# A SwiGLU kernel on one core: w2 in one load, the last token tile stored as 384 and 128 columns

## The chip, the cores and the metric

One Trainium2 chip, one core. The metric is the device time of one execution in microseconds (us); the time of a kernel is the median of several executions. TensorE does the matrix products, ScalarE the sigmoid and some of the copies out of PSUM, VectorE the multiplications and the rest of the copies, and SyncE's queue (SP) issues nearly all DMA transfers.

## The reference

```
B, S, D, F = 32, 32, 512, 1792        # x [B,S,D], w1 and w3 [D,F], w2 [F,D], all bf16
gate = einsum("bsd,df->bsf", x, w1)
up   = einsum("bsd,df->bsf", x, w3)
h    = silu(gate) * up
out  = einsum("bsf,fd->bsd", h, w2)   # 1024 tokens x 512
```

## The kernel before

The 1024 tokens stand in two blocks of 512 (`NB`) for the projections and in eight tiles of 128 (`NT`) for the output. F is cut into 14 pieces of 128 (`FT`).

**Loads.** At the start SP issues, in program order: a part of x, the first three F pieces of w1 and w3, a transposing load of x (line 78), the rest of w1 and w3 in three steps (`load_w`, line 66), a second transposing load for token block 1 (line 82), and last w2 in two halves of seven F pieces each (lines 84 and 85). Two loads go through ScalarE's queue. That makes 16 loads.

**Projections.** For each token block and each F piece, four matmuls make `gate_ps` and four make `up_ps` (`project`, line 123); `swiglu` takes the sigmoid on ScalarE (line 133) and multiplies twice on VectorE (lines 135 and 136) into `hT`, which holds h with F on the partitions.

**Output.** For each token tile `nt`, 14 matmuls (line 176) add up 128 tokens x `DB` columns in one PSUM tile `o_ps`, `hT` being the stationary operand and `w2_sb` the moving one. For the first seven tiles `DB` is 512, ScalarE casts `o_ps` to bf16 in `o_sb` (line 187), and SP stores it (line 188, 128 KB). The last tile is done in three pieces of 256, 128 and 128 columns, one after the other, each with its own 14 matmuls, a cast on VectorE (line 185) and a store (64, 32 and 32 KB). That makes ten stores, 26 transfers in all.

**What sets the order.** The program is in manual order: each engine runs its instructions in the order written, and waits on semaphores where it needs another engine's result. The `o_sb` tiles rotate over three buffers, so a cast also waits for the store that last used its buffer; the `o_ps` tiles rotate over four PSUM buffers. The DMA transfers take eight completion semaphores in turn, in program order: the first transfer takes semaphore 0, the ninth takes semaphore 0 again, and each transfer waits until the one eight before it has landed. These semaphores are called lane 0 to lane 7 below.

**The end.** After the last store SP waits for all lanes. This is a row of five wait instructions on SP (line 218 in the profile), with up to two semaphores each. In the program of the kernel before they are, in order: lane 3; lanes 4 and 2; lanes 5 and 1; lanes 6 and 0; lane 7 and VectorE. A drain and a barrier of all engines follow, and the span ends.

Of the kernel before, what the change touches and what calls it, by code (L numbers as in the profile page):

```python
# [10 lines left out]
def kernel(  # L11
# [8 lines left out]
    nc = tc.nc  # L20
# [5 lines left out]
    B, S, D = x.shape  # L26
# [5 lines left out]
    FT = F // P  # L32
# [8 lines left out]
    w2_v = w2.rearrange("(ft p) d -> p ft d", p=P)  # L41
# [14 lines left out]
    w2_sb = consts.tile([P, FT, D], bf16, name="w2_sb")  # L56
# [23 lines left out]
        load_w(nc.sync, w1_sb, w1_v, c0, c1)  # L80
        load_w(nc.sync, w3_sb, w3_v, c0, c1)
    nc.sync.dma_start_transpose(out=xT[:, :, NB:N], in_=x_flat[NB:N, :])
    FH = FT // 2
    nc.sync.dma_start(out=w2_sb[:, 0:FH, :], in_=w2_v[:, 0:FH, :])
    nc.sync.dma_start(out=w2_sb[:, FH:FT, :], in_=w2_v[:, FH:FT, :])

    def bank(name, tag="any"):
        return psum.tile([P, NB], fp32, name=name, tag=tag)
# [81 lines left out]
    for nt in range(NT):  # L170
        last = nt == NT - 1
        c0 = 0
        for DB in (D // 2, D // 4, D // 4) if last else (D,):
            o_ps = psum.tile([P, DB], fp32, name="o_ps", tag="any")
            for fo in range(FT):
                nc.tensor.matmul(  # L176
                    o_ps[:],
                    lhsT=hT[:, fo, nt * P : (nt + 1) * P],
                    rhs=w2_sb[:, fo, c0 : c0 + DB],
                    start=(fo == 0),  # L180
                    stop=(fo == FT - 1),
                )
            o_sb = work.tile([P, DB], bf16, name="o_sb", tag="o_sb")
            if last:
                nc.vector.tensor_copy(o_sb[:], o_ps[:])  # L185
            else:
                nc.scalar.copy(o_sb[:], o_ps[:])  # L187
            nc.sync.dma_start(
                out=out_flat[nt * P : (nt + 1) * P, c0 : c0 + DB],
                in_=o_sb[:],  # L190
            )
            c0 += DB
# [30 lines left out]
```

## Time and profile before

| what | value |
|---|---|
| median of five executions | 82.9 us |
| the five executions | 82.66, 82.71, 82.90, 83.63, 84.78 us |
| the profiled execution's own time | 83.63 us |
| its span | 81.8 us (81.84 in the trace) |
| TensorE busy | 76.3 us, 93% of the span |
| VectorE, ScalarE busy | 40.5 us, 22.9 us |
| granted TensorE clock | full in every slice |
| DMA moved | 7.67 MB |

The span is what the profile sees of the device's work. The profiled execution's own time is 1.79 us longer (83.63 - 81.84), which lies around it. That execution is also 0.73 us above the median of the five. A busy TensorE is a modelled figure, since matmuls are pipelined: the pace of the matmuls is read from the distance between their starts.

### The profile page before, as it was taken

The page shows a single profiled execution, that of the slowest core. Times are in us where ns is not written, and L with a number is a line of the kernel's source. Part 1 is how long each engine was busy: PE and PEld are TensorE (multiplying, and loading weights), DVE is VectorE, ACT ScalarE, POOL GpSimd, SP SyncE. Part 2 cuts the span into 40 slices and gives each one's busy share as a digit, 9 for nine tenths or more (in the row PEclk, how much of TensorE's full clock was granted, in tenths as well). Part 3 has the DMA queues.
Part 4 walks back from the last instruction along what each step waited for, and adds up shares of the span by engine and source line. Part 5 has one row for each costly group of instructions (what it writes and reads, how often), then busy time and mean ns, then how long its engine had stood idle before and what let it go on. Part 6 is the DMA issues. An engine that isn't in the chain of part 4 may idle for free.

```text
span 81.8 us, 1049 instructions
## 1 busy us (share of the span) xinstructions
PE 76.3 (93%) x396; PEld 38.1 (47%) x402; DVE 40.5 (49%) x62; ACT 22.9 (28%) x39; POOL 0.7 (1%) x6
## 2 busy tenths in 40 slices
PE   6989949999999999999999999999999999999960
PEld 2468714444444444444444444444444444444850
DVE  0130699678878778788788887883000000000040
ACT  4410721442224432234322244220220220220200
POOL 3000000000000000000000000000000000000000
PEclk9999999999999999999999999999999999999999
DMA  1999999978991000000000000000011012011120
GB/s 17 308 287 300 345 334 346 170 167 209 347 342 39 0 0 0 0 0 0 0 12 0 0 0 0 0 4 0 0 64 64 15 50 72 24 41 64 40 72 16
DMA packets 10949, 7.67 MB, mean 94 GB/s; under 512 B 3776, under 2 KB 10944, under 8 KB 10944
## 3 DMA queue, kind: packets, MB, share of 16 engines
q1 hardware_dynamic: 10528, 7.28, 32.9%
q10 hardware_dynamic: 416, 0.33, 1.2%
q8 instruction: 3, 0.05, 0.2%
q14 instruction: 2, 0.02, 0.1%
HBM read 5.77 MB, written 1.05 MB: 83 GB/s over the span
## 4 chain that ended last, share of the span: by engine, by line
PE 81%; DMA 9%; SPq 4%; issue 1%; DVE 0%; DVEq 0%
PE o_ps L176 30%; PE up_ps L123 26%; PE gate_ps L123 25%; DMA w_sb<-in_w_dram 9%; SPq L66 2%; SPq L78 2%; SPq L62 0%; DVE o_sb L185 0%; DVEq L185 0%
## 5 line engine op out<-in xcount | busy, mean ns | idle before, releaser
L123 PEld LDWEIGHTS <-w_sb 128*128 128x128 bf16 x248 | 24.0, 98 | 26.1 <-DMA w_sb<-in_w_dram 2.5
L123 PE MATMUL gate_ps<-xT,w_sb 128*128 128x512 bf16 (+1 forms) x122 | 28.7, 358 | 1.3 <-DMA w_sb<-in_w_dram 1.2
L123 PE MATMUL up_ps<-xT,w_sb 128*128 128x512 bf16 (+1 forms) x122 | 28.7, 358 | 0.5 <-DMA w_sb<-in_w_dram 0.5
L133 ACT ACTIVATE sig<-gate_ps 128x512 f32<-128x512 f32 x28 | 16.7, 597 | 33.2 <-PE gate_ps L123 33.2
L176 PE MATMUL o_ps<-w_sb,hT 128*128 128x512 bf16 (+2 forms) x138 | 24.3, 336 | 0.1
L135 DVE TENSOR_TENSOR t<-gate_ps,sig 128x512 f32<-128x512 f32 x28 | 19.3, 691 | 9.9 <-ACT sig L133 9.9
L136 DVE TENSOR_TENSOR hT<-t,up_ps 128x512 bf16<-128x512 f32 x28 | 19.3, 688 | 2.9
L176 PEld LDWEIGHTS <-hT 128*128 128x128 bf16 x140 | 12.6, 98 | 12.0
L185 DVE CAST o_sb<-o_ps 128x128 bf16<-128x128 f32 (+1 forms) x3 | 1.0, 337 | 22.3 <-PE o_ps L176 22.3
L187 ACT CAST o_sb<-o_ps 128x512 bf16<-128x512 f32 x7 | 4.1, 586 | 17.9 <-PE o_ps L176 17.9
L94 PE MATMUL warm_ps<-const-bfloat16-1.0 128*128 128x512 bf16 x6 | 2.7, 623 | 0.8 <-PEq L207 0.8
L116 DVE CAST xT<-pT 128x256 bf16<-128x256 f32 (+1 forms) x3 | 1.1, 380 | 3.8 <-PE pT L106 3.7
L74 ACT ACT_TABLE_LOAD x1 | 1.3, 1283 | 1.2 <-PEq L207 1.2
L94 PEld LDWEIGHTS <-const-bfloat16-1.0 128*128 128x128 bf16 x6 | 0.7, 133 | 1.9 <-issue 1.9
L106 PEld LDWEIGHTS <-x_sb 128*128 128x128 bf16 x8 | 0.8, 135 | 0.8 <-DMA x_sb<-in_x_dram 0.8
L106 PE MATMUL pT<-ident,x_sb 128*128 128x128 bf16 x8 | 1.1, 307 | 0.0
L116 ACT CAST xT<-pT 128x128 bf16<-128x128 f32 (+1 forms) x2 | 0.6, 319 | 1.3 <-PE pT L106 1.3
masks.py:199 POOL TENSOR_SCALAR_AFFINE_SELECT ident<-ident 128x128 bf16<-128x128 bf16 x1 | 0.3, 292 | 0.1
masks.py:197 POOL MEMSET ident<- 128x128 bf16 x1 | 0.2, 204 | 0.3 <-POOLq L207 0.3
L74 ACT ACTIVATE table<-const-bfloat16-1.0 128x1 f32<-128x1 bf16 x1 | 0.2, 202 | 0.0
L207 POOL MEMSET const-uint8-127<- 128x1 uint8 x1 | 0.1, 103 | 0.0
L207 POOL MEMSET const-bfloat16-1.0<- 128x1 bf16 x1 | 0.1, 102 | 0.0
(2 smaller groups left out, 0.2 us busy)
## 6 DMA issues: line engine op xcount, KB each, us to landing
w_sb<-in_w_dram SPq DMA_DIRECT2D x4, 512.0 KB, 7.8
w_sb<-in_w_dram SPq DMA_DIRECT2D x2, 896.0 KB, 6.9
out_dram<-o_sb SPq DMA_DIRECT2D x7, 128.0 KB, 1.7
w_sb<-in_w_dram SPq DMA_DIRECT2D x2, 384.0 KB, 8.6
w_sb<-in_w_dram SPq DMA_DIRECT2D x3, 192.0 KB, 3.9
w_sb<-in_w_dram ACTq DMA_DIRECT2D x1, 192.0 KB, 3.8
x_sb<-in_x_dram ACTq DMA_DIRECT2D x1, 128.0 KB, 2.7
x_sb<-in_x_dram SPq DMA_DIRECT2D x1, 128.0 KB, 2.6
```

The source lines that it names most:

```text
L66: queue.dma_start(out=w_sb[:, d0:d1, f0:f1], in_=w_v[:, d0:d1, f0:f1])
L74: nc.scalar.activation(table[:], one, SIGMOID)
L78: nc.sync.dma_start_transpose(out=xT[:, :, HB:NB], in_=x_flat[HB:NB, :])
L94: nc.tensor.matmul(warm_ps[:, 0:cols], lhsT=one.to_broadcast([P, P]), rhs=one.to_broadcast([P, cols]), start=True, stop=True,)
L106: nc.tensor.matmul(pT[:, i, j, :], lhsT=x_sb[:, nt, dt * P : (dt + 1) * P], rhs=ident[:], start=True, stop=True,)
L116: copy(xT[:, dts[0] : dts[-1] + 1, nts[0] * P : (nts[-1] + 1) * P], pT[:].rearrange("p d t c -> p d (t c)"),)
L123: nc.tensor.matmul(ps[:, c0 : c0 + n1 - n0], lhsT=w_sb[:, dt, fo * P : (fo + 1) * P], rhs=xT[:, dt, n0:n1], start=(dt == 0), stop=(dt == D ...
L133: nc.scalar.activation(sig[:], gate_ps[:], SIGMOID)
L135: nc.vector.tensor_mul(t[:], gate_ps[:], sig[:])
L136: nc.vector.tensor_mul(hT[:, fo, nb * NB : (nb + 1) * NB], t[:], up_ps[:])
L176: nc.tensor.matmul(o_ps[:], lhsT=hT[:, fo, nt * P : (nt + 1) * P], rhs=w2_sb[:, fo, c0 : c0 + DB], start=(fo == 0), stop=(fo == FT - 1),)
L187: nc.scalar.copy(o_sb[:], o_ps[:])
```

## The change

The two loads of w2 become one load of 1,792 KB. The last token tile is done in two pieces, of 384 and 128 columns, instead of three. The first piece is cast by ScalarE, as the tiles before it are; only the last piece (`c0 > 0`) is cast by VectorE. There are 15 loads and nine stores, 24 transfers in all. Lines after the w2 load stand two lines earlier in the changed kernel.

```diff
@@ -80,9 +80,7 @@
         load_w(nc.sync, w1_sb, w1_v, c0, c1)
         load_w(nc.sync, w3_sb, w3_v, c0, c1)
     nc.sync.dma_start_transpose(out=xT[:, :, NB:N], in_=x_flat[NB:N, :])
-    FH = FT // 2
-    nc.sync.dma_start(out=w2_sb[:, 0:FH, :], in_=w2_v[:, 0:FH, :])
-    nc.sync.dma_start(out=w2_sb[:, FH:FT, :], in_=w2_v[:, FH:FT, :])
+    nc.sync.dma_start(out=w2_sb[:], in_=w2_v)
@@ -170,7 +168,7 @@
     for nt in range(NT):
         last = nt == NT - 1
         c0 = 0
-        for DB in (D // 2, D // 4, D // 4) if last else (D,):
+        for DB in (D - D // 4, D // 4) if last else (D,):
             o_ps = psum.tile([P, DB], fp32, name="o_ps", tag="any")
             for fo in range(FT):
                 nc.tensor.matmul(
@@ -181,7 +179,7 @@
                     stop=(fo == FT - 1),
                 )
             o_sb = work.tile([P, DB], bf16, name="o_sb", tag="o_sb")
-            if last:
+            if c0 > 0:
                 nc.vector.tensor_copy(o_sb[:], o_ps[:])
             else:
                 nc.scalar.copy(o_sb[:], o_ps[:])
```

## The prediction

> **What bounds the kernel now.** I read the engines' shares first, then the chain of work that ended last, then the groups of instructions by shape, then the last six microseconds in stretches, and last SP's end-of-kernel waits. The page:
>
> ```profile
> span 81.8 us, 1049 instructions
> ...
> PE 76.3 (93%) x396; PEld 38.1 (47%) x402; DVE 40.5 (49%) x62; ACT 22.9 (28%) x39; POOL 0.7 (1%) x6
> ...
> PE 81%; DMA 9%; SPq 4%; issue 1%; DVE 0%; DVEq 0%
> PE o_ps L176 30%; PE up_ps L123 26%; PE gate_ps L123 25%; DMA w_sb<-in_w_dram 9%; SPq L66 2%; SPq L78 2%; SPq L62 0%; DVE o_sb L185 0%; DVEq L185 0%
> ```
>
> TensorE carries 81% of the chain, and its clock is granted in full in every slice. The other parts are the load of the first weights, before TensorE is fed, and a tail: the chain's last row ends with the VectorE cast of the last piece at 79.44 us, so 2.4 us follow in which only a store and the closing waits run. A change can move the span in three places: the head (not touched here), the pace of the matmuls, the tail.
>
> The groups by shape (line, engine, operation, count; then busy us and mean ns of one) give the durations used below:
>
> ```profile
> L187 ACT CAST o_sb<-o_ps 128x512 bf16<-128x512 f32 x7 | 4.1, 586 | 17.9 <-PE o_ps L176 17.9
> ...
> L185 DVE CAST o_sb<-o_ps 128x128 bf16<-128x128 f32 x2 | 0.6, 292 | 0.8 <-PE o_ps L176 0.8
> L185 DVE CAST o_sb<-o_ps 128x256 bf16<-128x256 f32 x1 | 0.4, 425 | 21.5 <-PE o_ps L176 21.5
> L116 ACT CAST xT<-pT 128x256 bf16<-128x256 f32 x1 | 0.4, 372 | 0.2 <-PE pT L106 0.2
> ```
>
> The busy time by stretch (us; then each engine's busy us and instructions, clock, DMA share, GB/s): the stage in which w2 arrives, then the last tile's pieces of 256, 128 and 128 columns, then the tail.
>
> ```profile
> 17.00:26.00 9.00, 8.95 (x43) 4.04 (x42) 7.22 (x11) 2.98 (x5) 0.00 (x0) 1.00 0.85 250
> 75.80:77.33 1.53, 1.53 (x15) 1.36 (x14) 0.00 (x0) 0.59 (x1) 0.00 (x0) 1.00 0.00 0
> 77.33:78.11 0.78, 0.78 (x16) 0.78 (x14) 0.42 (x1) 0.00 (x0) 0.00 (x0) 1.00 0.50 168
> 78.11:78.90 0.79, 0.79 (x17) 0.77 (x14) 0.29 (x1) 0.00 (x0) 0.00 (x0) 1.00 0.02 5
> 78.90:81.84 2.94, 0.16 (x3) 0.00 (x0) 0.29 (x1) 0.00 (x0) 0.00 (x0) 1.00 0.17 43
> ```
>
> TensorE is never idle until the last matmul: the pieces follow each other at full pace, and the casts and stores of earlier pieces lie beside it. Last, SP's waits after the last store, in two stretches (79.8 to 80.95 and 80.95 to 81.1):
>
> ```profile
> L218 SPq EVENT_SEMAPHORE  x3: 17/28/957, 79.8 to 80.0; - x3
> ...
> L218 SPq EVENT_SEMAPHORE  x2: 28/28/28, 81.0 to 81.0; - x2
> L218 SPq DRAIN  x1: 7/7/7, 81.1 to 81.1; - x1
> ```
>
> The third wait is the one that took 957 ns: lanes 5 and 1, and the last store is on lane 1. It ends at 80.925, 23 ns after the store's last landing at 80.902. Two waits already satisfied still follow it, at 80.961 and 81.023, and the drain comes at 81.088.
>
> **The change part by part.**
>
> *w2 in one load: 0.* The halves are issued at 17.30 and 17.93 (0.58 and 0.56 us on SP) and land at 23.29 and 25.77; the first matmul that reads w2 starts at 54.65. The cover is 28.9 us of projections. One load is one issue less; its length on SP lies between one half's 0.58 us and, if the queue holds it back as it held the second transposing load, that row's 6.26 us. I take 1.1. SP has nothing else until 58.5, so both ends cost nothing. The bytes are the same, and TensorE was busy for 8.95 of 9.00 us while they came. The rule that speaks for this part is in the Trainium skill, "DMA: Bandwidth & Descriptors", under Measured (HBM→SBUF): batch to 1 MiB or more for 75% of peak. It would make the load faster, and 28.9 us of cover make that worth nothing. TensorE's separate wait for the second half, before the eighth matmul of tile 0, goes too; the starts around it are 216 ns apart like all others, so it cost nothing.
>
> *Matmuls of the last tile: -0.04 us.* The starts are 215.8 ns apart for 512 columns, 109.1 for 256 (14 in 75.804 to 77.332) and 55.9 for 128. That is a line with 0.417 ns per column, so 384 columns are an estimated 162.4 ns. Before: 14 x (109.1 + 55.9 + 55.9) = 3.092 us. After: 14 x (162.4 + 55.9) = 3.056. Saving 0.036 us, all on the path. Bounds: 0 (if the narrow pieces hid a fixed part) to 0.1.
>
> *Cast and store of the 384 piece: 0, beside the last piece's matmuls.* The piece's last matmul falls due at 75.804 + 14 x 0.1624 = 78.08; its signal comes 0.178 us later, as for the other pieces, so 78.26; the cast starts at 78.32. ScalarE's casts took 266 (another row of that view), 372 and 586 ns for 128, 256 and 512 columns, hence an estimate of 479 for 384; it ends at 78.80. Its drain and barrier row just move later (76.64 to 78.80, still ahead of VectorE's). SP issues the store at 78.83 and is free, with its next lane wait, at 79.22. The new wait here is SP's on ScalarE, and only the last store is queued behind it. That store is due when the last cast ends: last matmul group through at 78.86, signal 79.04, cast 79.115 to 79.41, issue 79.435. Cover: 0.21 us. If the cast took the 512 row's 586 ns, SP would be free at 79.33, still in time.
>
> Here a rule speaks against the change: "ScalarE: Activation LUTs", Rules for kernel authors, wants elementwise work on VectorE, up to about three times faster per element in bf16. The rows say otherwise for these fp32 reads from PSUM: VectorE took 292 and 425 ns for 128 and 256, so an estimated 558 for 384 against ScalarE's 479. By the rule the cast would be up to 0.3 us shorter on VectorE, by the rows 0.08 longer; with 0.21 us of cover the sum is the same either way.
>
> *Last piece: unchanged length.* VectorE's 128-column cast 292 ns, issue 333 ns, landing 1.43 us after issue (79.470 to 80.902). The 384 store's packets are the neighbours to watch. In the trace packets start 0.83 us after issue; 64 KB moved in 0.36 us, 128 KB in 0.53, so 96 KB in an estimated 0.44: 79.66 to 80.10. The last store's begin at 79.435 + 0.83 = 80.265. Gap 0.165 us: no delay. Landing 80.87 instead of 80.90, which is the 0.036 again. Bounds: 0 to +0.44, as though the whole 96 KB lay ahead.
>
> *One store less: 0.* The skill ("DMA: Bandwidth & Descriptors", Anatomy of one DMA) puts a fixed 2.0 us on each transfer on GpSimd's path, and its rules ask to coalesce what is under 64 KB. Read as a serial price, a store less would be worth 2 us. But the last three stores were issued at 78.04, 78.69, 79.47 and landed at 79.58, 80.14, 80.90: their latencies overlap, and only the last counts.
>
> *The waits after the last store: -0.13 us.* With 24 transfers the last store is number 24, on lane 7. In the changed program SP's five closing waits are: lanes 3 and 2; 4 and 1; 5 and 0; 6 and VectorE; 7 and ScalarE. The lane that lands last is now in the last wait. Lane 6, the 384 store, lands at about 80.45, in good time. From landing to drain it was 81.088 - 80.902 = 0.186 us; now 0.023 to the wait's end and 0.037 to the drain, 0.060. Saving 0.126. Bounds: 0 to 0.19.
>
> **Sum** against the profiled execution: 81.84 - 0.036 - 0.126 = 81.68 us of span, and 83.63 - 0.16 = 83.47 with what lies around it. That execution was 0.73 us above the median of the runs shown; carried to the median, 82.90 - 0.16 = 82.74, forecast **82.75 us**. A measurement of this kernel can tell about 1% (0.83 us) from no change, so this is "within 1%".
>
> **The rivals.**
>
> 1. *Nothing but the pace (0.17):* the closing waits are not what the barrier waits for, or the 384-column matmuls are dearer than the line. For: 0.126 us hangs on one row of SP. Against: after it the drain and the barrier come at once. 82.87 to 82.90 us.
>
> 2. *Slower, the 96 KB store in front of the last one (0.05):* place, the 16 DMA engines after 79.66; the last store's packets stand behind a store three times as large as its old neighbour's 32 KB. Price up to 0.44 us: 82.74 + 0.44 = 83.2. It decides once the 96 KB move later or longer by 0.165 us than estimated, and makes the kernel slower than before from 0.33. Against: 128 KB took only 0.53.
>
> 3. *Transfers have a serial price (0.02):* a store less gives 2 us, 80.9. Against: the overlapping landings above.
>
> 4. *The change does its part, but the executions scatter (0.06):* the five shown reach from 82.66 to 84.78, and a median of a few can fall on 83.5 or more.
>
> **How the numbers follow.** The forecast has 0.70. The range starts from the lowest time shown, 82.66 - 0.16 = 82.5, less 0.1 for the bounds of waits and pace: 82.4. Upward it takes rival 2's 83.2 and some of the scatter: 83.3. Faster by over 1% is rival 3 and a little scatter, 0.03; slower by over 1% is most of rival 4, 0.05; within 1%, 0.92.
>
> **What would show it.** 14 matmuls of 128x384 with starts 162 ns apart; a ScalarE cast of about 480 ns that ends before 78.9; last store issued near 79.43 and landed near 80.87; the long closing wait as the fifth of five on SP, with the drain within 0.04 us of its end; span near 81.7. It is wrong if the last store takes over 1.6 us to land, if a wait for w2 stands ahead of the first line 174 matmul, or if waits follow the long one.

## The result, and the profile after

| what | before | after |
|---|---|---|
| median of all executions | 82.88 us (80 executions; 82.13 to 85.12) | 82.98 us (43 executions; 82.24 to 84.74) |
| ratio after/before | | 1.0004, 95% interval 0.9986 to 1.0022 |
| span of the profiled execution | 81.84 us | 80.51 us |

The time did not change by anything that this comparison can tell. The forecast was 82.75 us, "within 1%", and the time lies in the range of 82.4 to 83.3 us. The ratio leaves out executions that lay more than 1.5% above the fastest of their kernel. The two profiled spans differ by 1.33 us all the same, and most of this section is about why that is no gain. The page of the kernel after:

```profile
span 80.5 us, 1014 instructions
...
PE 76.7 (95%) x382; PEld 37.7 (47%) x388; DVE 39.5 (49%) x60; ACT 23.4 (29%) x40; POOL 0.7 (1%) x6
...
PE 95%; issue 1%; DVE 0%; DVEq 0%
PE gate_ps L121 31%; PE o_ps L174 30%; PE up_ps L121 30%; PE warm_ps L92 3%; PE pT L104 1%; DVE o_sb L183 0%; DVEq L183 0%
```

The chain has lost its DMA part (9% before). The reader might think that the change made a load of weights faster. But it touches no load that stands in that part. In the profiled execution before, the projections waited for weights. The waits in the first 13 us, before and then after, say how long (us in total, times, longest us):

```profile
PEld L123 <- DMA w_sb<-in_w_dram: 2.5, 3, 1.0
PE gate_ps L123 <- DMA w_sb<-in_w_dram: 1.2, 2, 0.8
PE up_ps L123 <- DMA w_sb<-in_w_dram: 0.5, 1, 0.5
```
```profile
PEld L121 <- DMA w_sb<-in_w_dram: 0.5, 1, 0.5
```

Cut by stage, the two traces differ like this. The first output matmul starts at 54.652 before and 53.459 after (-1.193 us, the head). From it to the last matmul's start it is 24.188 and 24.152 (-0.036). From there to the end of the span it is 3.001 and 2.903 (-0.098). The last two are what the change did.

The head differs by one load. The timelines show the first `up_ps` matmul of 512 columns, before and then after (start us, us):

```profile
12.34 0.39 PE L123 MATMUL up_ps<-xT,w_sb 128*128 128x512 bf16 x1 [0.47 <-DMA w_sb<-in_w_dram]
```
```profile
11.14 1.04 PE L121 MATMUL up_ps<-xT,w_sb 128*128 128x512 bf16 x4
```

It reads w3's fourth to seventh F pieces. That load was issued at 4.65 us before and at 4.78 after, and landed at 12.292 and 11.099, 1.193 us apart. The matmul followed 46 ns later in both traces, and from it to the first output matmul both took 42.314 us. So the whole difference of the head is that landing. The load is the same instruction in both programs and is issued ahead of everything that the change touches; whether two executions of one program differ as much is a question for experiments.

The groups by shape of the kernel after (line, engine, operation, count; busy us and mean ns of one):

```profile
L174 PE MATMUL o_ps<-w_sb,hT 128*128 128x384 bf16 x14 | 2.4, 326 | 0.0
L174 PE MATMUL o_ps<-w_sb,hT 128*128 128x128 bf16 x14 | 0.9, 219 | 0.0
L185 ACT CAST o_sb<-o_ps 128x384 bf16<-128x384 f32 x1 | 0.5, 479 | 1.7 <-PE o_ps L174 1.7
L183 DVE CAST o_sb<-o_ps 128x128 bf16<-128x128 f32 x1 | 0.3, 291 | 23.0 <-PE o_ps L174 23.0
```

The cast of 384 columns took 479 ns, as estimated. The mean of a matmul is a modelled length; the starts are 162 to 163 ns apart. The busy time by stretch: w2's arrival, the piece of 384, the piece of 128, the tail.

```profile
16.00:25.00 9.00, 8.95 (x43) 4.05 (x43) 7.41 (x12) 2.98 (x5) 0.00 (x0) 1.00 1.00 249
74.61:76.88 2.27, 2.27 (x15) 1.37 (x14) 0.00 (x0) 0.59 (x1) 0.00 (x0) 1.00 0.17 58
76.88:77.67 0.79, 0.79 (x16) 0.77 (x13) 0.00 (x0) 0.48 (x1) 0.00 (x0) 1.00 0.00 0
77.67:80.51 2.84, 0.16 (x3) 0.00 (x0) 0.29 (x1) 0.00 (x0) 0.00 (x0) 1.00 0.16 46
```

TensorE is as busy while w2 comes in one load as it was with two (8.95 of 9.00 us), and it has no gap in the last tile. SP's closing waits after the last store, in two stretches (78.6 to 79.0, 79.25 to 79.8):

```profile
L216 SPq EVENT_SEMAPHORE  x3: 28/28/28, 78.6 to 78.8; - x3
...
L216 SPq EVENT_SEMAPHORE  x2: 28/28/28, 79.3 to 79.7; - x2
L216 SPq DRAIN  x1: 7/7/7, 79.8 to 79.8; - x1
```

No wait lasts long any more in the record. Instead there is a hole of 0.4 us ahead of the fifth, which starts at 79.701, 16 ns after the last store's landing at 79.685, and one of 0.5 us ahead of the fourth, which starts 17 ns after the landing of the 384 store. Nothing follows the fifth but the drain, at 79.766.

### The profile page after: what moved, and what is told of

Its sections match the earlier page's. It is cut to its first block, busy times and chain, and to the rows that moved or that the text cites. A ratio compares the mean times of both kernels' runs of the same rounds, so it can differ in the third digit from the quotient of the medians.

```text
span 80.5 us, 1014 instructions
## 1 busy us (share of the span) xinstructions
PE 76.7 (95%) x382; PEld 37.7 (47%) x388; DVE 39.5 (49%) x60; ACT 23.4 (29%) x40; POOL 0.7 (1%) x6
## 4 chain that ended last, share of the span: by engine, by line
PE 95%; issue 1%; DVE 0%; DVEq 0%
PE gate_ps L121 31%; PE o_ps L174 30%; PE up_ps L121 30%; PE warm_ps L92 3%; PE pT L104 1%; DVE o_sb L183 0%; DVEq L183 0%
## 5 line engine op out<-in xcount | busy, mean ns | idle before, releaser
L121 PE MATMUL gate_ps<-xT,w_sb 128*128 128x512 bf16 (+1 forms) x122 | 29.2, 364 | 0.2
L174 PEld LDWEIGHTS <-hT 128*128 128x128 bf16 x126 | 11.8, 98 | 12.7
L185 ACT CAST o_sb<-o_ps 128x512 bf16<-128x512 f32 (+1 forms) x8 | 4.6, 573 | 19.6 <-PE o_ps L174 19.6
```

The costliest lines, as they stand in the source:

```text
L121: nc.tensor.matmul(ps[:, c0 : c0 + n1 - n0], lhsT=w_sb[:, dt, fo * P : (fo + 1) * P], rhs=xT[:, dt, n0:n1], start=(dt == 0), stop=(dt == D ...
L174: nc.tensor.matmul(o_ps[:], lhsT=hT[:, fo, nt * P : (nt + 1) * P], rhs=w2_sb[:, fo, c0 : c0 + DB], start=(fo == 0), stop=(fo == FT - 1),)
```

## The experiments

Two theories were at stake. Theory P is the prediction's sum, part by part. Its rival, N, is that the sum does not reach the whole time. The executions of one kernel are spread over some 3 us, so to see 0.1 us the cause of that scatter had to be found first.

**A late start (four kernels).** All have this edit, and differ in the parts of the change that they hold.

```diff
-    keep_warm(6, NB)
+    keep_warm(6 + 48, NB)
```

The kernel before:

> The kernel before with 48 more warming matmuls (54 instead of 6) ahead of the first transposes; the extra ones only fill time. Theory S (the scatter of the executions is the arrival of the first weights): TensorE now starts on weights that have landed, so the executions agree within 0.2 us (before: 82.13 to 85.12), at about 91 us (48 x 0.216 = 10.4 us more, less the stalls of the head). Rival (scatter arises in the tail or outside the span): the executions still reach over 2 us. From the last matmul's start to the end of the span: 3.00 us as before.

The kernel after:

> The changed kernel with the same 48 extra warming matmuls. Theory P (the prediction's sum): 0.16 us below the kernel before with the late start (0.036 from the matmuls, 0.126 from the closing waits), and from the last matmul's start to the end 2.88 us. Rival N (the sum is not in the time, since the barrier or what lies around the span takes it back): within 0.05 us of it.

Only w2 in one load (`nc.sync.dma_start(out=w2_sb[:], in_=w2_v)` in place of the two halves):

> Late start; of the change only w2 in one load: 25 transfers, last tile still 256, 128, 128; the last store is on lane 0, which stands in the fourth of the five closing waits, with one more behind it. Theory P: 0.06 us below the kernel before with the late start, all of it one closing wait. If one load of w2 matters by itself: anything else than -0.03 to -0.10.

Only the last tile in two pieces (the change with w2's two halves put back):

> Late start; of the change only the last tile in 384 and 128 with ScalarE's cast, w2 in two loads: 25 transfers; the last store is on lane 0, which here stands in the third closing wait, with two behind it. Theory P: 0.04 us below the kernel before with the late start, from the 14 matmuls less alone. Rival C (the 96 KB store delays the last one): 0 to 0.3 us above.

Theory S (the scatter is the arrival of the first weights) fell as the only cause. The six executions of each still scatter: 92.03 to 93.59, 91.91 to 93.44, 92.43 to 93.50, and 91.93 to 93.47 us, so their medians (93.11, 92.90, 93.02 and 92.12 us) tell nothing of 0.1 us. No trace of the four shows a wait for weights. In these kernels the cause is TensorE's pace at the start. The warming matmuls by stretch of two microseconds (us; busy us and count of those that run in it; clock, DMA, GB/s), in the kernel with w2 in one load and in the one with the tail alone:

```profile
1.00:3.00 2.00, 2.00 (x6) 1.00 0.52 144
3.00:5.00 2.00, 2.00 (x7) 1.00 1.05 338
5.00:7.00 2.00, 2.00 (x7) 1.00 1.15 265
7.00:9.00 2.00, 2.00 (x11) 1.00 1.03 328
```
```profile
1.00:3.00 2.00, 2.00 (x6) 1.00 0.45 125
3.00:5.00 2.00, 2.00 (x10) 1.00 1.08 357
5.00:7.00 2.00, 2.00 (x11) 1.00 1.00 239
7.00:9.00 2.00, 2.00 (x11) 1.00 0.97 299
```

The same instructions start 427 ns apart at first and 219 ns apart later. The first start at the full pace is at 6.67 us in the one and at 3.65 in the other, and the first gate matmul then starts at 16.160 and 14.679. The clock column reads 1.00 all the while; the count tells it. (That the kernels took 93 us and not the expected 91 or so has the same reason: of the 54 warming matmuls of the kernel before, the first 12 ran at half pace.) The Trainium skill, "TensorE: Matmul & The Clock Gate", Part 1, has the rule behind this row: the array starts at half clock and is released after a window of some 3.4 us of activity, and the window runs freely, so its phase differs between executions. The times here fit it: the full pace comes 2.9 to 5.9 us after the first warming matmul at 0.77 us, a spread of 3.0. Every microsecond of half pace costs about half a microsecond of work: 3.02 us later at full pace, 1.48 us later at the first gate matmul.

After that start all four kernels are the same to a nanosecond up to the output stage: from the first gate matmul to the first output matmul 48.406, 48.406, 48.405 and 48.405 us. So the traces give each part of the change by itself (us):

| late start | first to last output matmul | closing waits behind the one that ends last | last matmul's start to the end |
|---|---|---|---|
| before | 24.187 | 2 | 3.009 |
| after | 24.152 | 0 | 2.918 |
| w2 in one load | 24.188 | 1 | 2.955 |
| tail in two pieces | 24.152 | 2 | 3.019 |

Having 14 matmuls less gives 0.035 us. One load of w2 gives nothing of its own: it moves the last store by one lane, and so shortens the closing waits by one. One store less, in the last row, gives nothing beside the matmuls. The 96 KB store costs the last one at most 0.01 us.

The whole times say the same once the start is taken off each profiled execution (us):

| late start | first start at full pace | first gate matmul | that execution's time | time less that start |
|---|---|---|---|---|
| before | 5.42 | 15.568 | 92.96 | 77.39 |
| after | 5.34 | 15.491 | 92.75 | 77.26 |
| w2 in one load | 6.67 | 16.160 | 93.50 | 77.34 |
| tail in two pieces | 3.65 | 14.679 | 92.04 | 77.36 |

The change is worth 0.13 us here, the load of w2 0.05 and the tail 0.03, each from one execution.

**A fixed start (six kernels).** The projections are made to begin at a time that ScalarE sets, so that it does not matter when the pace doubles:

```diff
+    pad = consts.tile([P, NB], fp32, name="pad")
+    for _ in range(9):
+        nc.scalar.activation(pad[:], one.to_broadcast([P, NB]), SIGMOID)
+    ident2 = consts.tile([P, P], bf16, name="ident2")
+    nc.scalar.copy(ident2[:], ident[:])
...
-                    rhs=ident[:],
+                    rhs=ident2[:],
...
-    keep_warm(6, NB)
+    keep_warm(20, NB)
```

The kernel before:

> The kernel before with a fixed start: 20 warming matmuls, and beside them nine dependent 512-column sigmoids on ScalarE, whose end a copy of the identity waits for; TensorE's first transpose reads that copy. So the projections start at a time that ScalarE sets (about 9 us) and not at one that depends on when TensorE's pace doubles. Theory G (the scatter is the moment at which the pace doubles): the executions agree within 0.3 us, near 86.5 us, and from the first gate matmul to the first output matmul it takes 48.4 us as in all four late kernels. Rival (something else scatters): they still reach over 1.3 us.

The kernel after:

> The changed kernel with the same fixed start. Theory P: 0.13 to 0.16 us below the kernel before with the fixed start, and resolved if theory G holds; rival N (no gain in the whole time): within 0.05 us.

The kernel before with w2 in eight loads:

```diff
+    for f0, f1 in ((0, 2), (2, 4), (4, 6), (6, 8), (8, 10), (10, 12), (12, 13), (13, 14)):
+        nc.sync.dma_start(out=w2_sb[:, f0:f1, :], in_=w2_v[:, f0:f1, :])
```

> Fixed start, the kernel before with w2 in eight loads instead of two: 32 transfers, the last tile still 256, 128, 128; the last store is on lane 7, alone with VectorE in the fifth closing wait. Theory P: the closing waits' part alone, 0.09 to 0.13 us below the kernel before with the fixed start, from the last matmul's start to the end 2.91 us; and eight small loads of w2 cost nothing. If the number of transfers has a price of its own, it is slower than that kernel (0.33 us of issue each, six more).

The kernel after with w2 in three loads (0 to 5, 5 to 10, 10 to 14):

> Fixed start, the changed kernel with w2 in three loads: 26 transfers again, so the last store is on lane 1, in the second of the five closing waits, with three behind it. Theory P: 3 x 0.062 less the 0.022 by which a wait ends sooner when its second semaphore is the late one, about 0.15 to 0.19 above the changed kernel with the fixed start: 86.85 to 86.89 us, all of it between the last store's landing and the drain. Rival (the pieces and not the lane make the gain): 86.70, equal to it.

The scatter is gone, so theory G (the scatter is the moment at which the pace doubles) holds: 86.81 to 86.84, 86.69 to 86.71, 86.72 to 86.74 and 86.88 to 86.89 us. The traces show why: the full pace came at 3.56 us in the kernel before and at 6.27 in the kernel after, and both started the first transpose at 8.709. (One execution of each of the first three kernels, and two of the one at 480 columns below, lay 1.66 us higher, at a mean granted clock of 0.98; they are left out here, and the last section comes back to them. The profile of the kernel before is of such an execution, with full clock again long before the tail.) Now 0.02 us can be told:

| fixed start | transfers | waits behind the one that ends last | last matmul's start to the end | median |
|---|---|---|---|---|
| before | 26 | 2 | 2.999 | 86.83 |
| after | 24 | 0 | 2.907 | 86.70 |
| before, w2 in eight loads | 32 | 0 | 2.905 | 86.74 |
| after, w2 in three loads | 26 | 3 | 3.062 | 86.88 |

The whole change is worth 0.13 us of the whole time (86.83 to 86.70), and so theory P holds against rival N. The lane alone is worth 0.09 (86.83 to 86.74), with six loads more and the old pieces, so six loads under cover cost nothing that shows. Put back on lane 1, the changed kernel loses 0.18 us and is slower than the kernel before: lane 1 stands in its second closing wait, and three follow. Of the 0.18, 0.155 lie behind the last matmul's start. Another 0.02 lie ahead of the first transpose (8.730 against 8.709 us); this kernel and the two with the casts exchanged below ran on another chip than the rest of these experiments. SP's closing waits in these kernels, in the table's order without the first (count; shortest, median and longest ns):

```profile
L221 SPq EVENT_SEMAPHORE  x5: 28/28/28, 83.0 to 84.1; - x5
L221 SPq DRAIN  x1: 7/7/7, 84.2 to 84.2; - x1
```
```profile
L222 SPq EVENT_SEMAPHORE  x5: 17/28/28, 83.0 to 84.1; - x5
L222 SPq DRAIN  x1: 7/7/7, 84.2 to 84.2; - x1
```
```profile
L222 SPq EVENT_SEMAPHORE  x5: 28/28/1012, 83.0 to 84.3; - x5
L222 SPq DRAIN  x1: 7/7/7, 84.3 to 84.3; - x1
```

The drain comes at 84.2 us in the first two and at 84.3 in the third, where a wait of 1012 ns stands second and three of 28 ns each still follow it.

**Where the cover on SP ends.** The kernel after with the fixed start and the last tile cut at 480:

```diff
-        for DB in (D - D // 4, D // 4) if last else (D,):
+        for DB in (D - D // 16, D // 16) if last else (D,):
```

> Fixed start, the changed kernel with the last tile cut at 480 and 32 instead of 384 and 128. Theory P (SP's order is the cover that must hold): the 480 cast takes 586 x 480/512, some 0.56 us, and its store's issue 0.33, while the last piece's 14 matmuls are short, so the last store stands behind the first on SP: issue to issue 0.40 us or so, and the end 0.4 us later than with 384 and 128 (0.3 above the kernel before). If that cover does not matter: 0.2 to 0.3 below the changed kernel, since the last cast and store are smaller.

It took 87.18 us, 0.48 more than with 384 and 128; 0.4 was expected. The timelines of the tail, at 480 and 32 and then at 384 and 128 (start us, us, engine, line, operation):

```profile
82.07 0.56 ACT L190 CAST o_sb<-o_ps 128x480 bf16<-128x480 f32 x1 [2.25 <-PE o_ps L179]
82.42 0.19 DVE L188 CAST o_sb<-o_ps 128x32 bf16<-128x32 f32 x1 [23.13 <-PE o_ps L179]
82.66 0.81 SPq L191 DMA_DIRECT2D out_dram<-o_sb  x2
```
```profile
81.52 0.48 ACT L190 CAST o_sb<-o_ps 128x384 bf16<-128x384 f32 x1 [1.69 <-PE o_ps L179]
82.02 0.94 SPq L191 DMA_DIRECT2D out_dram<-o_sb  x2
82.31 0.29 DVE L188 CAST o_sb<-o_ps 128x128 bf16<-128x128 f32 x1 [23.02 <-PE o_ps L179]
```

At 480 the last cast ends at 82.615, but SP is still bound to the first store: it starts that issue at 82.657, and the last store goes out at 83.081, 0.466 us after its data were ready. At 384 it goes out at 82.631, 0.027 after the cast. So the cover that the prediction named is real: SP is free at 82.419 there, 0.21 us ahead of need. The 0.48 us is not that wait alone. The last store goes out 0.44 us later behind its cast and takes 0.02 longer to land. The last cast is 0.10 shorter, but it starts 0.12 later after the first output matmul: the 32-column matmuls start 25 ns apart, where the prediction's line would give 16.

**The casts exchanged (two kernels).** The kernel after, with 384 columns on VectorE and the last 128 on ScalarE, with the fixed start and with the kernel's own:

```diff
-            if c0 > 0:
+            if last and c0 == 0:
```

> Fixed start, the changed kernel with the two casts of the last tile exchanged: 384 columns on VectorE (an estimated 558 ns), the last 128 on ScalarE (266 instead of 292 ns, and its cast starts 67 instead of 77 ns after TensorE's signal). Theory P: 0.036 us below the changed kernel with the fixed start, 86.66, since the 384 store, due 0.09 us later, still leaves SP before the last store is due. If the skill's rule held (VectorE up to three times faster), the 384 cast would be 0.2 us or less; the rows say 0.56.

> The changed kernel, own start, with the casts exchanged as in the kernel before this one. 0.04 us is expected beside the changed kernel, and 0.17 beside the kernel before; executions that scatter by over 1 us will not show it: within 0.5% of the kernel before.

With the fixed start it took 86.69 us (86.68 to 86.70), 0.01 below the kernel after; its first transpose started 0.02 us later in the trace, and from the last matmul's start to the end it took 2.878 us against 2.907. So the gain is 0.03 us, by those rows: the 0.01 and the 0.02 of the later start. Expected was 86.66. With its own start it took 82.81 us, at a ratio of 1.0000 to the kernel before (0.9970 to 1.0031): not to be told. The timeline of the fixed start has the reason:

```profile
81.55 0.56 DVE L188 CAST o_sb<-o_ps 128x384 bf16<-128x384 f32 x1 [22.23 <-PE o_ps L179]
82.14 0.81 SPq L191 DMA_DIRECT2D out_dram<-o_sb  x2
82.32 0.27 ACT L190 CAST o_sb<-o_ps 128x128 bf16<-128x128 f32 x1 [2.47 <-PE o_ps L179]
```

The 384 cast took VectorE 0.56 us where ScalarE took 0.48, and the last one 0.27 on ScalarE where VectorE took 0.29. The shorter one counts, since it is last. Of the versions tried this is the shortest in the tail. The rule that the prediction set against ScalarE ("ScalarE: Activation LUTs" of the Trainium skill, Rules for kernel authors) names relu, max, min, add and mul in bf16; for this cast of fp32 out of PSUM its factor did not show.

## Why the prediction was right or wrong

- **The verdict, "within 1%", was right**, and for the reason given: two small savings at the end, nothing else. The fixed start measures -0.13 us where the sum said -0.16. The plain comparison alone would not have shown that: no gain at all would have been "within 1%" too, and the measured 82.98 us lies 0.23 above the forecast, more than the whole effect. That a time so scattered fell in the range is in part luck.
- **Matmuls of the last tile, -0.036:** measured -0.034 to -0.036 in three pairs of traces. The line through the three widths held for 384 columns: 162 to 163 ns. It does not reach down to 32 (25 ns).
- **The closing waits, -0.126: right in mechanism, too large in size.** Measured -0.09 to -0.10 from the last matmul's start to the end. Two terms were off. The prediction let the wait end 23 ns after the landing, as before. It ends 44 ns after (79.685 to 79.729). In all the traces it is 22 to 23 ns where the lane that lands last is the second of its wait's two semaphores, and 44 to 45 where it is the first; the latter is always lane 7 in the fifth wait, so which of these matters is not shown. And the last store took 1.444 us to land where the row before had 1.432. 0.126 - 0.021 - 0.012 is 0.093.
- **Rival 1, nothing but the pace:** excluded, since the lane alone gives 0.09 us with the old pieces.
- **Cast and store of the 384 piece, 0:** right row by row. The cast took 479 ns (estimate 479), its store landed 1.626 us after issue, and SP was free before the last store was due. The 480 cut shows what the last store loses without that cover: 0.44 us.
- **w2 in one load, 0; one store less, 0:** right. The load was on SP for 0.58 us (the prediction took 1.1) and landed 8.8 us after issue, at 24.99, against a first use at 53.5. It was not faster for being one: the two halves took 8.5 us from the first issue to the last landing. Rival 3, a serial price of transfers that makes a store less worth 2 us, is excluded by the kernel with the tail alone: a store less there gave nothing but the matmuls' 0.035. (The kernel with 32 transfers cannot exclude it, since its six loads more lie under the projections.)
- **Rival 2, the last store behind the 96 KB:** did not happen. The last store landed 1.436 to 1.453 us after issue with 96 KB in front, and 1.432 to 1.446 with 32 KB. The small difference goes with the lane: 1.432 to 1.436 on lane 1, whatever is in front, and 1.442 to 1.453 on lanes 0 and 7.
- **Rival 4, scatter:** it is what the plain comparison sees. A gain of 0.13 us is a ratio of 0.9984, just below the interval's lower end of 0.9986. So the plain executions did not show it. Over all executions the means are 83.03 us before and 83.04 after, and the standard error of their difference is 0.12, so a gain of 0.13 is neither shown nor excluded. Nothing before the load of w2 differs between the programs, and the late and the fixed start both show the gain, so I take the difference for scatter of the head. That the head's mean is the same in both plain kernels was not shown. Nor was it shown how much of the plain scatter is the pace and how much the weights' landing.
- **Span near 81.7:** wrong for the profiled execution (80.51), by 1.19 us in the head. The prediction took the head of one execution for a constant. In these two traces one load of w3, the same in both programs, landed 1.193 us apart.

## What to carry to other kernels

Before a gain of tenths is looked for, find what scatters at the start and pin it; the tail of a trace can be read to nanoseconds even where whole times cannot. A last store should land on the completion semaphore that the closing waits ask for last: each wait behind it costs 0.04 to 0.06 us here, and a load more or less anywhere in the program moves it. When a last tile is cut in two, the first part's cast and issue must be over before the second part's cast ends (at 384 and 128 by 0.21 us), or the small last store waits on SP.

## What the runs showed of the hardware

- TensorE's pace doubles at a time that differs between executions: between 3.56 and 6.67 us from the start of the span in the ten traces with longer warming, with the matmuls 427 ns apart until then. The granted clock in the profile's rows reads 1.00 for that time; only the distance of the starts shows it.
- In the kernel before with the fixed start TensorE idled for 2.14 us ahead of the first transpose (6.57 to 8.71 us). The profiled execution then ran at half clock for 3.41 us, from 10.24 to 13.65, here by the granted clock as well. From the first gate matmul to the first output matmul it took 50.07 us instead of 48.41, and 88.49 us in all where the others took 86.83. The Trainium skill's page "TensorE: Matmul & The Clock Gate" names some 3.4 us of idle time (Part 1), or 3 (Why this matters for your kernels), as what brings the half clock back. Here less stood ahead of it, in the one such execution that has a trace; idle times of 0.75 to 1.66 us in the other five traces did not bring it. Five of the 36 executions with the fixed start were longer by the same 1.66 us. That the idle time is the cause was not tested.
- Matmuls of 32 columns start 25 ns apart, those of 128, 256, 384 and 480 columns 56, 109, 162 and 203 ns.
- With the start pinned, executions of a whole kernel of 87 us agree within 0.03 us, those five left out.

The rows of TensorE between 11 and 13 us that show the half clock, in that execution of the kernel before and then in the kernel after with the fixed start (us; busy us and count; clock, DMA, GB/s):

```profile
11.00:13.00 2.00, 2.00 (x12) 0.50 1.10 330
```
```profile
11.00:13.00 2.00, 2.00 (x21) 1.00 1.10 330
```
